# Stage one in the program's own order on ScalarE and VectorE, with the square written straight into the high half

## The chip, the cores and the metric

The kernel runs on one core of a Trainium2 chip. The metric is the time of one execution on the device in microseconds; for the kernel before, three executions have a median of 5993.0 us (5985.8 to 5993.41). The engines are named as in the profile: PE is TensorE's matrix multiply and PEld its weight load, DVE is VectorE, ACT is ScalarE, POOL is GpSimd, SP is SyncE, which here issues nearly all DMAs.

## The reference

Three computations run one after the other. The shapes are 8 batches of 3072 rows, 256 columns, and 64 columns for `z`.

```python
scores = (1.0 / S) * np.matmul(z, z.transpose(0, 2, 1))
attn = np.maximum(scores, 0.0) ** 2
x = (u * np.matmul(attn, v)).reshape(B * S, D)       # 24576 rows of 256
h = x @ w_in                                         # w_in: 256 x 2048, float64
x2 = np.maximum(0.01 * h, h) @ w_out                 # w_out: 2048 x 256, float64
# then: a gate gives every row of x2 to one of 8 experts, 3072 rows each,
# and each expert computes max(rows @ w1[e], 0) @ w2[e]
```

The third computation is the second stage of the kernel (`part_b`), which the change leaves alone.

## The kernel before

All matrix products are made of float32 data split into two halves that TensorE multiplies fast: `hi` is the value rounded on a copy to the type `float32r`, `lo` is the value minus `hi`, and a product is the sum of hi by hi, lo by hi and hi by lo. The helper `split` (line 336) does this: ScalarE copies into `hi` (line 337), VectorE subtracts for `lo` (line 338).

Stage one is `part_a`. Its work is 48 chunks of 512 rows, 6 to a batch. Each chunk has an attention half (class `Attn`) and an MLP half (class `Mlp`). The list `units` (lines 582 to 587) cuts them up: an attention half is 12 units of two key blocks each, an MLP half is 8 units of two blocks of 128 hidden columns each. The order is attention of chunk c, then the MLP of chunk c-1, then attention of chunk c+1, and so on; the very first two attention halves stand together.

Every unit has two parts. In `s1`, TensorE makes a tile of scores `s` (attention) or of hidden values `h` (MLP) in PSUM, and ScalarE and VectorE turn it into `hi` and `lo`. In `s2`, TensorE multiplies `hi` and `lo` into the accumulators `acc0` and `acc1`. The loop at line 647 calls `s1` of unit n and then `finish`, which calls `s2` of unit n-2, so the elementwise work of a unit has the matrix work of two other units beside it.

What ScalarE and VectorE do for one unit of attention: ScalarE writes `r` = relu of `s` (line 467). Then the square: in the first two chunks, and in 3 of 12 units (`k % 8 == 4`) of the others, by ScalarE in place (line 469); otherwise by VectorE as `s` times `r` (line 471). Then `split` into `hi` and `lo`. For one unit of the MLP: ScalarE writes 0.01 `h` (line 521), VectorE the maximum with `h` (line 522), then `split`.

Beside that there are smaller jobs, which come from `after` and `prefetch`, or before the loop: splitting the keys (`load_z`), the queries (`queries`) and the values (`load_v`) of chunks and batches to come, each behind a DMA; taking the accumulators out (`out_of`, lines 442 to 445, marked high priority); `ready`, which splits the result of attention for the MLP; and the gate's logits. The logits of a chunk are 32 VectorE instructions of line 575, two to an item of the list `side`, followed by one item of `rt.choose` with 5 small instructions; `after` takes three items at an MLP unit. In the first chunks `load_w` also converts the 16 pieces of the float64 weights to float32 by integer operations on VectorE (lines 375 to 381), two GpSimd operations (lines 382 and 383), ScalarE's high half and GpSimd's low half.

What sets the order. TensorE runs in the order in which the program calls it (`manual_schedule(engines={PE})`, line 841). The order on ScalarE, VectorE, GpSimd and the DMA queues is chosen by the scheduler of the framework when the kernel is built, from its own model of the times, under the dependencies between tiles; the order on an engine is then fixed, and at run time each engine takes its instructions one after the other.

Of the kernel before, what the change touches and what calls it, by code (L numbers as in the profile page):

```python
# [9 lines left out]
F32 = mybir.dt.float32  # L10
# [300 lines left out]
def part_a(nc, tc, uT, v, zT, w_in, w_out, wgT, x2d, L, rt):  # L311
# [12 lines left out]
    with ExitStack() as st:  # L324
# [20 lines left out]
        def load_w(piece):  # L345
            f, out = divmod(piece, 2)
            f *= 2
            W = cv.tile([128, 512], F32, name='cW')
# [11 lines left out]
            for half, c, x in src:  # L360
# [17 lines left out]
            V.scalar_tensor_tensor(W, lsw, 2.0 ** -52, P.bitcast(F32), op0=ALU.mult, op1=ALU.mult)  # L378

# [3 lines left out]
            nc.gpsimd.tensor_mul(W, W, P.bitcast(F32))  # L383
            split(hi, lo, W.rearrange("p (a d) -> p a d", **shape), nc.gpsimd)
# [17 lines left out]
        def load_z(b, g):  # L402
# [6 lines left out]
            split(k[:, 0], k[:, 1], zr)  # L409

        def queries(b, q):
# [6 lines left out]
            split(*x, zr)  # L418
            return x

        def load_v(b, g):
# [4 lines left out]
            split(vh, vl, raw)  # L426
            VH[b, g], VL[b, g] = vh, vl

        def halves(r):
            hi = wk.tile([128, 2, CH], F32R, tag='hi', name='hi', bufs=3)  # L430
            lo = wk.tile([128, 2, CH], F32R, tag='lo', name='lo', bufs=3)
            split(hi, lo, r)
            return hi, lo
# [8 lines left out]
        def out_of(acc, to):  # L442
            with tc.high_priority():
                nc.scalar.activation(to, acc[:, 1], AF.Copy)
                nc.vector.tensor_add(to, acc[:, 0], to)  # L445

        class Attn:

            def __init__(self, b, q):
                self.b, self.q = b, q  # L450
                self.xs, self.y = [], [None] * KT

            def prep(self):
                b, q = self.b, self.q
                self.z = Q.pop((b, q)) if (b, q) in Q else queries(b, q)

            def s1(self, k):
                if k == 0:
                    self.prep()
# [8 lines left out]
                if at.index(self) < 2 or k % 8 == 4:  # L468
                    nc.scalar.activation(r, r, AF.Square)
                else:  # L470
                    nc.vector.tensor_mul(r, s, r)  # L471
                return halves(r)

            def s2(self, k, hl, d):
# [13 lines left out]
                if k == NKB - 2:  # L488
                    self.y[d] = kv.tile([128, CH], F32, tag='raw', name='y', bufs=3)
                    out_of(self.acc[d], self.y[d])  # L490
                    if d == KT - 1:
                        for i, y in enumerate(self.y):
                            nc.vector.scalar_tensor_tensor(self.x[:, i], y, 1.0 / (S * S), self.x[:, i], op0=ALU.mult, op1=ALU.mult)
# [14 lines left out]
        class Mlp:  # L508
# [4 lines left out]
            def s1(self, f):  # L513
# [9 lines left out]
                return halves(r)  # L523

            def s2(self, f, hl, d):
# [12 lines left out]
                if f == FT - 2:  # L538
                    self.rows(d)

            def rows(self, d):
                if not lgt:
                    logit_tiles()
# [45 lines left out]
        Q = {(0, 0): queries(0, 0)}  # L589
        for g in range(NG):  # L590
            if g * G * 128 % CH == 0:
                load_z(0, g * G * 128 // CH)
            load_v(0, g)
            if g == 1:
                Q[0, 1] = queries(0, 1)
        q, piece = [], 0

        pending = []

        def finish():  # L600


            u, k, hl = q.pop(0)
            end = NKB if isinstance(u, Attn) else FT
            ends = end - 4 if isinstance(u, Mlp) else 0
            if k == ends:
                u.s2(k, hl, 0)
                pending.append((u, k, hl))
            else:
# [270 lines left out]
```

## Time and profile before

| | |
|---|---|
| median of three executions | 5993.0 us |
| the profiled execution | 6009.63 us |
| its span, first to last instruction | 6007.9 us |
| TensorE matmul busy (PE) | 5540.0 us, 92% |
| VectorE busy (DVE) | 3922.1 us, 65% |
| ScalarE busy (ACT) | 2739.6 us, 46% |
| GpSimd busy (POOL) | 497.0 us, 8% |
| mean granted TensorE clock | 0.968 |

In the rows further below, a line of a group names the line of the kernel, the engine, the operation, what it writes and reads, the shapes and the count; then the busy time in us and the mean duration of one in ns; then how long the engine was idle just before these instructions and which instruction ended that idle time. In a timeline, the first column is the start in us from the start of the span and the second the duration; a bracket at the end holds the idle time of the engine before the instruction and what ended it. `L436` is the helper `mm`, through which all matmuls of stage one go; an `x2` on a matmul is its pair for the two halves of the array.

### The profile page before, as it was taken

To read this page: it belongs to the slowest core of one execution; us is meant where nothing else is said; L and a number is where in the kernel's file an instruction comes from. 1 tells how busy PE (TensorE), PEld (TensorE's weight loads), DVE (VectorE), ACT (ScalarE), POOL (GpSimd) and SP (SyncE) were. 2 spreads that over 40 slices of the span, in tenths; PEclk is the share of its full clock that TensorE was granted. 3 is DMA by queue.
4 is the path that set the end of the run, shared out by engine and by line. 5 is a ranking of instruction groups with operands and counts; after the bars stand their busy time and mean duration, and the time that the engine had idled before them with its cause. 6 is when DMAs were issued, how large, how long until landed. Compare 5 with 4: busy or idle time off the path is not lost. (4 is left out here: it accounts for less than half of the span.)

```text
span 6007.9 us, 122714 instructions
## 1 busy us (share of the span) xinstructions
PE 5540.0 (92%) x53466; PEld 4782.2 (80%) x53466; DVE 3922.1 (65%) x8179; ACT 2739.6 (46%) x3172; POOL 497.0 (8%) x466
## 2 busy tenths in 40 slices
PE   5999999899989999999999999999998599999999
PEld 3877788787878778787787778878787488888898
DVE  8566666766666666666666666676666766767532
ACT  4555555555554555545555554555543122222232
POOL 5000000000000000000000000000000232323332
PEclk7999999999999999999999999999999799999999
DMA  3011110101111011111101111010110111111211
GB/s 105 21 33 43 33 30 25 54 17 33 33 43 33 17 42 35 32 33 34 42 17 33 47 29 33 22 54 19 31 31 15 40 53 50 57 50 55 70 46 36
DMA packets 147533, 229.19 MB, mean 38 GB/s; under 512 B 21936, under 2 KB 87472, under 8 KB 144816
## 3 DMA queue, kind: packets, MB, share of 16 engines
q1 hardware_dynamic: 124032, 153.15, 9.3%
q0 software_dynamic: 20736, 67.13, 3.2%
q8 instruction: 418, 6.85, 0.5%
q10 hardware_dynamic: 2224, 1.06, 0.1%
q14 instruction: 123, 1.01, 0.1%
HBM read 120.59 MB, written 50.33 MB: 28 GB/s over the span
## 5 line engine op out<-in xcount | busy, mean ns | idle before, releaser
L436 PE MATMUL acc<-lo,vh 64*128 64x512 f32 x4608 | 957.9, 408 | 209.3 <-DVE lo L338 209.2
L338 DVE TENSOR_TENSOR lo<-r,hi 128x1024 fp32r<-128x1024 f32 x576 | 707.1, 1228 | 556.2 <-ACT hi L337 556.2
L337 ACT ACTIVATE hi<-r 128x1024 fp32r<-128x1024 f32 x576 | 610.4, 1060 | 995.1 <-DVE r L471 989.0
L436 PE MATMUL acc<-hi,vh 64*128 64x512 f32 x4608 | 944.9, 403 | 74.7 <-DVE xt L445 36.2
L436 PE MATMUL acc<-hi,vl 64*128 64x512 f32 x4608 | 934.8, 398 | 0.0
L436 PE MATMUL acc<-woh,hi 64*128 64x256 f32 x6144 | 875.2, 281 | 0.8 <-DVE xt L445 0.6
L436 PE MATMUL acc<-woh,lo 64*128 64x256 f32 x6144 | 871.7, 280 | 0.2 <-DVE lo L338 0.2
L436 PE MATMUL acc<-wol,hi 64*128 64x256 f32 x6144 | 871.4, 280 | 0.0
L522 DVE TENSOR_TENSOR g<-h,g 128x1024 f32<-128x1024 f32 x384 | 469.9, 1224 | 447.7 <-ACT g L521 446.8
L436 PEld LDWEIGHTS acc<-lo,vh 64*128 64x128 f32 x4608 | 456.4, 191 | 373.6 <-DVE lo L338 291.1
L338 DVE TENSOR_TENSOR lo<-g,hi 128x1024 fp32r<-128x1024 f32 x384 | 470.5, 1225 | 421.8 <-ACT hi L337 421.8
L337 ACT ACTIVATE hi<-g 128x1024 fp32r<-128x1024 f32 x384 | 407.0, 1060 | 544.3 <-DVE g L522 543.5
L436 PE MATMUL h<-xh,wih 64*128 64x512 f32 x3072 | 611.1, 392 | 31.4 <-DVE g L522 31.4
L521 ACT ACTIVATE g<-h 128x1024 f32<-128x1024 f32 x384 | 393.7, 1025 | 503.6 <-PE h L436 503.1
L436 PEld LDWEIGHTS acc<-woh,hi 64*128 64x128 f32 x6144 | 587.4, 187 | 32.8 <-DVE y L445 18.0
L436 PEld LDWEIGHTS acc<-hi,vh 64*128 64x128 f32 x4608 | 458.1, 192 | 193.6 <-DVE xt L445 56.2
L436 PE MATMUL h<-xh,wil 64*128 64x512 f32 x3072 | 609.8, 391 | 0.0
L436 PE MATMUL h<-xl,wih 64*128 64x512 f32 x3072 | 606.5, 389 | 0.0
L436 PEld LDWEIGHTS acc<-wol,hi 64*128 64x128 f32 x6144 | 587.4, 187 | 13.2
L467 ACT ACTIVATE r<-s 128x1024 f32<-128x1024 f32 x576 | 583.0, 1012 | 12.2 <-PE s L436 12.2
L436 PEld LDWEIGHTS acc<-woh,lo 64*128 64x128 f32 x6144 | 587.3, 187 | 0.4 <-DVE lo L338 0.4
L767 ACT ACTIVATE bhi<-hb 128x512 fp32r<-128x512 f32 x384 | 228.7, 597 | 766.4 <-PE hb L764 579.5
(187 smaller groups left out, 9887.7 us busy)
## 6 DMA issues: line engine op xcount, KB each, us to landing
rawv<-in_v SPq DMA_DIRECT2D x96, 256.0 KB, 2.9
ut<-in_uT SPq DMA_DIRECT2D x48, 512.0 KB, 4.0
xh<-xh SPq DMA_DIRECT2D x192, 128.0 KB, 2.4
xl<-xl SPq DMA_DIRECT2D x192, 128.0 KB, 2.3
x_rows<-xt SPq DMA_DIRECT2D x48, 512.0 KB, 3.0
zq<-in_zT SPq DMA_DIRECT2D x96, 128.0 KB, 3.2
zr<-in_zT SPq DMA_DIRECT2D x96, 64.0 KB, 2.4
craw<-in_w_in SPq DMA_DIRECT2D x64, 64.0 KB, 2.3
```

The lines of the kernel that those rows point to most:

```text
L337: nc.scalar.activation(hi, src, AF.Copy)
L338: (eng or nc.vector).tensor_sub(lo, src, hi.bitcast(F32))
L436: nc.tensor.matmul(o, w[half], x[half], start=first, stop=last)
L467: nc.scalar.activation(r, s, AF.Relu)
L521: nc.scalar.activation(r, h, AF.Copy, scale=0.01)
L522: nc.vector.tensor_max(r, h, r)
L767: nc.scalar.activation(hi, h, AF.Relu)
```

## The change

It does three things, all in stage one.

First, ScalarE and VectorE join TensorE in the manual schedule: in stage one both run in the order in which the program calls them. SyncE's and GpSimd's orders stay with the scheduler.

Second, the loop is rewritten to that end. `s1` now only makes `r` (or `g`); a new method `halves` makes `hi` and `lo`. For unit n the order is: the loads due ahead (`ahead`), `s1` of n, `s2` of n-2, the first half of an accumulator that is done (`leave(0)`), `halves` of n, `leave(1)`, and then the small jobs that fall due (`todo`). Loads are split in two: the DMA is issued in `ahead`, and the function that it returns, the split, runs at the end of the next unit's work. The logits are taken at the MLP's units alone, one item between `hi` and `lo` in `halves`, two more in `todo`. A piece of weights is spread over four units, and its float32 buffer is doubled. The tables of the router (`rt.start`) and the gate's loads come at the seventh MLP unit.

Third, the square of chunks 2 to 47: ScalarE squares `r` straight into `hi` in every unit, VectorE squares `r` in place and then subtracts `hi` for `lo`. The separate square by ScalarE and its copy into `hi` are gone there, and VectorE no longer reads `s`.

The diff, with what the text speaks of:

```diff
         def load_w(piece):
-            W = cv.tile([128, 512], F32, name='cW')
+            W = cv.tile([128, 512], F32, name='cW', bufs=2)
...
+            yield
...
             V.scalar_tensor_tensor(W, lsw, 2.0 ** -52, P.bitcast(F32), op0=ALU.mult, op1=ALU.mult)
+            yield
...
             nc.gpsimd.tensor_mul(W, W, P.bitcast(F32))
+            yield
             split(hi, lo, W.rearrange("p (a d) -> p a d", **shape), nc.gpsimd)
...
-            split(k[:, 0], k[:, 1], zr)
+            return lambda: split(k[:, 0], k[:, 1], zr)
...
-            split(vh, vl, raw)
+            return lambda: split(vh, vl, raw)
...
                 nc.scalar.activation(r, s, AF.Relu)
-                if at.index(self) < 2 or k % 8 == 4:
+                return r
+
+            def halves(self, k, r):
+                hi, lo = new_halves()
+                if self.c < 2:
                     nc.scalar.activation(r, r, AF.Square)
+                    split(hi, lo, r)
                 else:
-                    nc.vector.tensor_mul(r, s, r)
-                return halves(r)
+                    nc.scalar.activation(hi, r, AF.Square)
+                    nc.vector.tensor_mul(r, r, r)
+                    nc.vector.tensor_sub(lo, r, hi.bitcast(F32))
+                return hi, lo
...
+            def halves(self, f, r):
+                hi, lo = new_halves()
+                nc.scalar.activation(hi, r, AF.Copy)
+                if f and side:
+                    side.pop(0)()
+                nc.vector.tensor_sub(lo, r, hi.bitcast(F32))
+                return hi, lo
...
+        def ahead(n, u, k):
+            i = k // 2
+            then = lambda step, f: todo.append((n + step, f))
+            if n < 2 * FT and (n % 2 or isinstance(u, Mlp)) and len(pieces) < FT:
+                w = load_w(len(pieces))
+                pieces.append(w)
+                next(w)
+                for step in (1, 2, 3):
+                    then(step, lambda: next(w, None))
+            if isinstance(u, Attn):
+                if u.c == 0:
+                    if i + 1 < NG:
+                        then(1, load_v(0, i + 1))
...
+                elif u.c > 1 and i in (3, 5):
+                    then(0, lambda: at[u.c - 1].ready(i // 4))
+                if u.q == NCH - 1 and u.b + 1 < B and i in (2, 4, 6, 8, 10, 11):
+                    then(1, load_v(u.b + 1, (i - 1) // 2))
                 return
+            for _ in range(2 if k else 0):
+                then(0, lambda: side and side.pop(0)())
+            if u.c == 0 and i == 6:
+                then(0, logit_tiles)
...
+            a = at[u.c + 1]
+            if i == 3 and a.c + 1 < len(at):
+                then(1, queries(at[a.c + 1].b, at[a.c + 1].q))
+            if a.q == NCH - 1 and a.b + 1 < B and i > 1:
+                then(1, load_v(a.b + 1, NG // 2 + i - 2))
+                then(1, load_z(a.b + 1, i - 2))
...
         for n, (u, k) in enumerate(units):
+            ahead(n, u, k)
+            r = u.s1(k)
+            out = finish() if len(q) > 1 else []
+            for f in out[:1]:
+                f()
+            q.append((u, k, u.halves(k, r)))
+            for f in out[1:]:
+                f()
+            for f in [f for m, f in todo if m <= n]:
+                f()
+            todo = [x for x in todo if x[0] > n]
...
-    with tc.manual_schedule(engines={mybir.EngineType.PE}):
+    with tc.manual_schedule(engines={mybir.EngineType.PE, mybir.EngineType.DVE, mybir.EngineType.Activation}):
         part_a(nc, tc, uT, v, zT, w_in, w_out, wgT, x2d, L, rt)
```

## Rows read from the trace of the kernel before

**Rows 1.** The page: busy time and share of the span of each engine.
```profile
PE 5540.0 (92%) x53466; PEld 4782.2 (80%) x53466; DVE 3922.1 (65%) x8179; ACT 2739.6 (46%) x3172; POOL 497.0 (8%) x466
```
**Rows 2.** Busy time of the engines in seven stretches.
```profile
core 0: us, PE busy (x) PEld busy (x) DVE busy (x) ACT busy (x) POOL busy (x), PEclk, DMA share, GB/s
321.00:361.70 40.70, 35.74 (x304) 27.58 (x302) 31.12 (x87) 22.97 (x24) 0.00 (x0) 1.00 0.07 21
361.70:406.50 44.80, 44.80 (x530) 39.64 (x528) 25.70 (x25) 19.87 (x23) 0.00 (x0) 1.00 0.06 13
406.50:413.60 7.10, 7.10 (x112) 6.84 (x110) 5.16 (x5) 4.53 (x6) 0.00 (x0) 1.00 0.58 152
6.00:145.70 139.70, 77.74 (x402) 53.84 (x404) 118.78 (x150) 65.97 (x85) 74.71 (x51) 0.72 0.34 101
145.70:221.20 75.50, 75.50 (x800) 65.00 (x800) 35.03 (x32) 46.89 (x49) 0.00 (x0) 1.00 0.12 30
150.00:4640.00 4490.00, 4227.31 (x44513) 3615.01 (x44510) 2989.37 (x5537) 2303.85 (x2491) 0.00 (x0) 0.98 0.12 32
4640.00:6008.00 1368.00, 1230.62 (x8519) 1109.82 (x8518) 811.30 (x2481) 364.81 (x592) 420.92 (x404) 0.95 0.15 50
```
**Rows 3.** Who PE waited for, 150 to 4640 us: total, times, longest.
```profile
PE acc L436 <- DVE lo L338: 188.9, 151, 2.8
PE acc L436 <- DVE xt L445: 36.8, 47, 0.8
PE h L436 <- DVE g L522: 31.4, 8, 5.5
```
**Rows 4.** Timeline around a gap of PE in chunk 3's attention half.
```profile
334.93 0.42 DVE L575 SCALAR_TENSOR_TENSOR junk<-xt,wg 128x256 bf16<-128x256 f32 x1
...
337.43 1.22 DVE L338 TENSOR_TENSOR lo<-r,hi 128x1024 fp32r<-128x1024 f32 x1
...
338.70 0.49 PE L436 MATMUL acc<-lo,vh 64*128 64x512 f32 x2 [2.79 <-DVE lo L338]
```
**Rows 5.** DVE's logits in the attention half from 321.0 to 361.7 us, grouped.
```profile
L575 DVE SCALAR_TENSOR_TENSOR junk<-xt,wg 128x256 bf16<-128x256 f32 x32 | 11.4, 416 | 0.0
```
**Rows 6.** TensorE's first `s2` matmul of a unit, where nothing stalls: units 0, 2, 6.
```profile
149.94 0.39 PE L436 MATMUL acc<-hi,vh 64*128 64x512 f32 x2
...
156.74 0.39 PE L436 MATMUL acc<-hi,vh 64*128 64x512 f32 x2
...
170.34 0.39 PE L436 MATMUL acc<-hi,vh 64*128 64x512 f32 x2
```
**Rows 7.** ACT's first result tile `y`, chunk 2 (280.8) to chunk 47 (4549.72).
```profile
L444 ACT ACTIVATE y<-acc x92: 577/586/595, 280.8 to 4550.2; 128x512 f32<-128x512 f32 x92
...
4549.72 1.07 ACT L444 ACTIVATE y<-acc 128x512 f32<-128x512 f32 x2
```
**Rows 8.** Durations of the elementwise operations, grouped by line and shape, whole span.
```profile
L338 DVE TENSOR_TENSOR lo<-r,hi 128x1024 fp32r<-128x1024 f32 x576 | 707.1, 1228 | 556.2 <-ACT hi L337 556.2
...
L467 ACT ACTIVATE r<-s 128x1024 f32<-128x1024 f32 x576 | 583.0, 1012 | 12.2 <-PE s L436 12.2
...
L471 DVE TENSOR_TENSOR r<-s,r 128x1024 f32<-128x1024 f32 x414 | 504.3, 1218 | 0.3 <-ACT r L467 0.3
...
L469 ACT ACTIVATE r<-r 128x1024 f32<-128x1024 f32 x162 | 171.9, 1061 | 5.0
...
L338 DVE TENSOR_TENSOR vl<-rawv,vh 128x512 fp32r<-128x512 f32 x96 | 69.1, 727 | 36.7 <-ACT vh L337 36.7
```
**Rows 9.** A batch boundary: timeline at the longest gap of PE.
```profile
580.65 0.63 ACT L337 ACTIVATE vh<-rawv 128x512 fp32r<-128x512 f32 x1 [3.10 <-DMA rawv<-in_v]
...
585.26 0.80 PE L436 MATMUL h<-xh,wih 64*128 64x512 f32 x2 [5.34 <-DVE g L522]
```
**Rows 10.** The start: two weight pieces in ScalarE's timeline.
```profile
73.60 0.63 ACT L337 ACTIVATE wih<-cW 128x512 fp32r<-128x512 f32 x1 [2.55 <-POOL cW L383]
...
80.85 0.63 ACT L337 ACTIVATE woh<-cW 128x512 fp32r<-128x512 f32 x1 [5.70 <-POOL cW L383]
```

More of the change, by code (lines that the diff above doesn't have):

```diff
@@ L417, in queries @@
             x = [wk.tile([128, CH], F32R, tag='x%s0' % n if b == q == 0 else 'q' + n, name='q' + n, bufs=1) for n in 'hl']
-            split(*x, zr)
-            return x
+            Q[b, q] = x
+            return lambda: split(*x, zr)
         def load_v(b, g):
@@ L425, in load_v, with new_halves @@
             vl = kv.tile([128, G, D], F32R, tag='vl', name='vl', bufs=NG)
-            split(vh, vl, raw)
             VH[b, g], VL[b, g] = vh, vl
[L429 to L433, printed above, removed]
+            return lambda: split(vh, vl, raw)
+        def new_halves():
+            return [wk.tile([128, 2, CH], F32R, tag=n, name=n, bufs=3) for n in ('hi', 'lo')]
         def mm(o, w, x, half, first, last):
@@ L487, in s2, with leave @@
                             mm(self.acc[d][:, j], w[:, i, c], a[:, i], half, k + i == n == 0, k + i == NKB - 1 and n == 2)
[L488 to L493, printed above, removed]
+            def leave(self, d):
+                y = self.y[d] = kv.tile([128, CH], F32, tag='raw', name='y', bufs=3)
+                out_of(self.acc[d], y)
+                if d == KT - 1:
+                    for i, y in enumerate(self.y):
+                        nc.vector.scalar_tensor_tensor(self.x[:, i], y, 1.0 / (S * S), self.x[:, i], op0=ALU.mult, op1=ALU.mult)
+                    if self.c in (0, len(at) - 1):
+                        for i in range(KT):
+                            self.ready(i, self.c > 0)
             def ready(self, k, last=False):
@@ L537, in s2, with leave @@
                                    f + i == FT - 1 and t % 2 == 1 and n == 2)
[L538 to L543, printed above, removed]
+            def leave(self, d):
                 lp, wg, j0 = lgt['pool'], lgt['wg'], self.c * TT
@@ L587, in part_a @@
         units += later
[L589 to L598, printed above, removed]
+        q, pending, todo, Q = [], [], [], {}
         def finish():
             u, k, hl = q.pop(0)
[L604 to L607, printed above, removed]
+            att = isinstance(u, Attn)
+            u.s2(k, hl, 0)
+            if k == (0 if att else FT - 4):
@@ L647, in part_a @@
[L647 to L657 removed]
+                return []
+            if pending:
+                w, j, h = pending.pop()
+                w.s2(j, h, 1)
@@ new lines, in part_a @@
+        pieces = []
+        for f in [queries(0, 0), load_z(0, 0)]:
+            f()
+        for f in (load_v(0, 0), load_z(0, 1)):
+            todo.append((0, f))
+        for n, (u, k) in enumerate(units):
+            ahead(n, u, k)
[7 more added lines that the diff above has]
+            for f in [f for m, f in todo if m <= n]:
+                f()
+            todo = [x for x in todo if x[0] > n]
@@ L658, in part_a @@
         while q:
-            finish()
+            for f in finish():
+                f()
         while side:
```

65 lines of the change are left out of this document (13 added, 52 removed).

## The prediction

> **What bounds the kernel now.** I read the busy shares first: TensorE's matmuls cover 92% of the span, VectorE 65%, ScalarE 46% [rows 1]. So TensorE sets the pace, and the question is where it stands still. The table of stretches answers that: from 150 to 4640 us PE is busy for 4227 of 4490 us; the second stage, behind 4640 us, is not touched by the change and keeps its 1368 us [rows 2]. The same table cuts one chunk: 40.7 us of attention half with 5.0 us in which PE is not even busy, then 44.8 us and 7.1 us with no idle time at all [rows 2]. All the loss of an ordinary chunk lies in the attention half.
>
> The waits say who is late: in stage one PE waited 188.9 us for VectorE's `lo`, 151 times, and 36.8 us for `xt`, once a chunk [rows 3]. The timeline shows why `lo` is late. Around the longest gap of a chunk VectorE does not idle: it works through logits (line 575), starts `lo` only at 337.43, and PE goes on at 338.70 after 2.79 us [rows 4]. In that attention half stand all 32 logits, 11.4 us [rows 5]. The scheduler put them, and the emptying of the accumulator behind some of them, ahead of work for which TensorE waits. Nothing is short of capacity: VectorE is busy for 25.7 of the MLP half's 44.8 us [rows 2].
>
> **What a chunk costs without stalls.** Units 0 to 6 of a stretch with no stall have their first `s2` matmul at 149.94 and 170.34: 3.40 us for an attention unit [rows 6]. The window of 40.7 us holds the matmuls of ten units, 34.0 us; so it loses 6.7 us, and the chunk of 92.6 us (40.7 + 44.8 + 7.1) could take 85.9 [rows 2, 6]. The mean chunk is longer than 92.6: from the first `y` of chunk 2 to that of chunk 47 are 45 chunks, (4549.72 - 280.8) / 45 = 94.86 us [rows 7]. The 2.2 us of difference are the batch boundaries (below) and a granted clock of 0.98 in the mean over the stage, against 1.00 in the chunk shown [rows 2]. In the start, where PE stands still for much of the time, the mean is 0.72, so part of it is spent at the lower of the two levels, 1.2 GHz [rows 2]; I take it that the lower level goes with the stalls.
>
> **The change, part by part.**
>
> The order of the logits. 16 items of two logits, 0.71 us each (11.4 / 16, [rows 5]), leave the attention half for the MLP half, one item between `hi` and `lo`, two behind the unit. VectorE's work in the MLP half becomes 25.7 + 11.4 + about 1 (`choose`) = 38 of 44.8 us [rows 2, 5]: it fits. In the attention half it becomes 31.1 - 13.9 (logits with their accumulator reads, and `choose`) + 3.7 (below) = 20.9 us for ten units of 3.40: it fits with a third to spare. So the 6.7 us go, if the fixed order makes no new wait.
>
> The square. Three units of twelve lose a ScalarE square of 1.06 us and gain a VectorE one of 1.22 [rows 8]: 3.7 us more on VectorE in a chunk, off TensorE's path. The chain of a unit was relu 1.01, square 1.22 on VectorE, `hi` 1.06, `lo` 1.23, together 4.5. It stays as long: VectorE squares `r` in place, and must wait until ScalarE has read it for `hi`; so again relu 1.01, `hi` 1.06, square 1.22, `lo` 1.23 [rows 8]. With four handovers of some 0.1 us I take 4.9. TensorE asks for it two units later, 6.8 us from the end of `s1` to `hi` (149.94 to 156.74) and about 0.45 more to `lo` [rows 6]: 2.3 us to spare. `s` in PSUM comes free earlier, since only the relu reads it; TensorE did not wait for that, so nothing is gained. The bounds of this edit are 0 and, if the chain came out of its cover, what it exceeds 7.2 us by.
>
> The fixed order. Each engine now holds what stands behind a waiting instruction. `leave(0)` stands ahead of `halves` on ScalarE, and waits for an `s2` that ends about 1.4 us after `s1`; relu covers 1.0 of it. Queued behind are `hi` and with it `lo`: 0.4 us late, out of 2.3 spare. `leave(1)` waits for the end of the unit's matmuls, when the next relu isn't due yet. At the end of the MLP the chain is tighter, since two short attention units follow, but by then the logits are used up (17 items, three at each unit after the first). I take no stall for an ordinary chunk; the upper bound, from the chunk's waits that don't concern logits, is 1 us.
>
> The batch boundary, 7 times. The values and keys of the next batch were split by ScalarE in a row, each behind its DMA: ScalarE held the MLP's relu back, and PE stood for 5.34 us [rows 9]; that wait came 8 times, 31.4 us in all [rows 3]. Now each MLP unit from the third takes one value and one key tile, with the DMAs issued a unit ahead on SP, but only three `raw` buffers. VectorE gets six value splits at 0.73 us [rows 8] and six key splits, which are half as large, at some 0.4: 38 + 6.8 = 44.8 us, as much as the MLP half lasts. So there the cover is used up. Between 0 and the roughly 10 us that such a chunk exceeds others by now, I take 3 us, near the lower end, since the work just fits: 7 x 3 = 21 us.
>
> The start. To 145.7 us PE is busy for 77.7 of 139.7 us at a granted clock of 0.72; from there to 221.2 it has no idle time [rows 2]. What blocks is ScalarE: it sat 5.70 us at a weight piece behind GpSimd [rows 10] with the relu of a unit behind it. With the pieces spread over four units each that chain runs beside the rest. The next limit is VectorE: 118.8 + 35.0 = 153.8 us of work up to 221.2 [rows 2], all of which remains. TensorE needs 75.5 us plus some 13 units of 3.40, 120. So stage one reaches the same point at 6 + 154 = 160 us instead of 221 if VectorE binds throughout (61 saved), at 127 if TensorE does (94). I take 60. At the worst SP, whose queue carries nine issues for each pair of pieces and the loads of values between, holds the splits back in fixed order, and 30 are left. The router's tables and the gate's loads move from the first microseconds to the seventh MLP unit; a few us, in that range.
>
> **The sum.** 46 chunks x (94.86 - 85.9) = 412 us; less 21 for the boundaries; plus 60 at the start: 451 us. Against the profiled execution's own 6009.6 us that makes 5559; this execution lies 16.6 us above the median of 5993.0, to which I apply the same gain: 5542 us. Its own bounds: all at best 412 + 94, 5487; all at worst 412 - 70 - 46 + 30 = 326, 5667.
>
> **The rivals.**
>
> Loads block the fixed order (A). ScalarE and VectorE in order stop at each split whose DMA is late, at the start and the boundaries; ordinary chunks gain, nothing else does. For it: one late split already stopped everything for 5 us [rows 9], and three buffers serve all loads. Against: loads are now issued a unit ahead and spread. 412 - 70 = 342 us gained: 5651.
>
> The gap is a matter of buffers (B). `r` and `s` have two buffers, `hi` and `lo` three; if these bound, a new order would leave the gaps. Only the start gains: 5993 - 60 = 5933. Against it: with the same buffers six units run without a stall [rows 6], and the wait ends with a `lo` that was queued, not one without room. The Trainium skill ("Perfetto Trace Analysis", section "Identifying the Most-Contended Engine" and what follows on strategy) has this as a rule: the same gap, repeated, can mean that there is no room for the next tile. The trace doesn't bear it out here.
>
> The MLP half becomes serial (C, slower). Place: the fixed order of VectorE and ScalarE in an MLP unit, with the logits in it. If max waits for ScalarE, `hi` for max, `lo` for `hi`, and nothing of another unit fills these waits, a unit takes 1.0 + 1.2 + 1.1 + 1.2 and three items, 2.1: 6.6 us, with the chunk's other jobs some 7.0, where TensorE needs 5.6 (44.8 / 8). Eight units lose 11 us, a chunk takes 97.1, and 46 x (97.1 - 94.86) - 60 = +43: 6036. It decides from 6.9 us a unit on. Against it: one item stands just where VectorE waits for `hi`, and relu and max belong to a unit that TensorE needs only two units later.
>
> The change doesn't do what it says (D): the order built is in effect the old one: 5993.
>
> **Chances.** Forecast 0.76, A 0.14, B 0.04, C 0.03, D 0.03. The range takes the forecast's own bounds and A: 5487 to 5680, 0.9 of the chance. A measurement of this kernel can tell 0.2%, 12 us, from no change. Faster is forecast, A and B, 0.94; same is D, 0.03; slower is C, 0.03.
>
> **What would show it.** Right: the same stretches of an attention half with PE busy throughout; no wait of PE for `lo` worth 10 us in all of stage one; logits between MLP operations; first `y` of one chunk to the next at about 86 us; granted clock near 1.00 there; the stretch of 75 us that ends the start reached some 60 us earlier. Wrong: waits of ScalarE for `rawv` or `zr` with PE idle behind them (A), gaps at the same units ended by a `lo` that started late though VectorE was free (B), PE waiting for `g` in every MLP unit (C). I would be most wrong by a stall that the new order makes in every unit: each 0.1 us of that is 0.1 x 20 x 46 = 92 us.

## The result and the profile after

The changed kernel takes 5559.9 us (median of four runs, 5557.7 to 5563.9) where the kernel before, beside it, takes 5991.5: a ratio of 0.928, 95% interval 0.9266 to 0.9298. The prediction was 5542 us in a range of 5487 to 5680; the forecast's case came, and no rival. The profiled executions differ by 6007.9 - 5560.2 = 447.7 us of span, where the sum of the prediction said 451. That agreement is better than its terms, and in part luck: one of them was a third too large, and another part was not foreseen.

Where the time went can be cut at two points that both traces have, the first and the last start of VectorE's part in emptying the MLP's accumulator (`xt`). Before, in the view of the tile `xt` (duration of one at least, in the middle and at most, then the first and the last start):

```profile
L445 DVE TENSOR_TENSOR xt<-acc,xt x96: 679/681/693, 227.9 to 4635.7; 128x512 f32<-128x512 f32 x96
```

And after:

```profile
L445 DVE TENSOR_TENSOR xt<-acc,xt x96: 681/683/692, 189.0 to 4199.6; 128x512 f32<-128x512 f32 x96
```

| part | before, us | after, us | gained | predicted |
|---|---|---|---|---|
| start, to the first `xt` | 227.9 | 189.0 | 38.9 | 60 |
| chunks, to the last `xt` | 4407.8 | 4010.6 | 397.2 | 412 - 21 = 391 |
| rest, mostly the second stage | 1372.2 | 1360.6 | 11.6 | 0 |

The busy shares, which answer [rows 1]: TensorE rises from 92% to 97% of a shorter span, and VectorE does more, not less, since it took over squares.

```profile
PE 5375.5 (97%) x53466; PEld 4707.5 (85%) x53466; DVE 4100.0 (74%) x8317; ACT 2644.1 (48%) x3034; POOL 501.6 (9%) x466
```

The table of stretches, which answers [rows 2]: the three pieces of an ordinary chunk (7.1 us from its first unit to its third, 34.1 us of ten attention units, 44.6 us of MLP half), then a batch boundary's MLP half, then the start in two pieces and all chunks.

```profile
core 0: us, PE busy (x) PEld busy (x) DVE busy (x) ACT busy (x) POOL busy (x), PEclk, DMA share, GB/s
1904.50:1911.60 7.10, 7.10 (x112) 6.84 (x110) 4.42 (x5) 5.51 (x6) 0.00 (x0) 1.00 0.01 2
1911.60:1945.70 34.10, 34.10 (x306) 28.18 (x306) 26.56 (x24) 22.46 (x23) 0.00 (x0) 1.00 0.26 71
1945.70:1990.30 44.60, 44.60 (x532) 39.77 (x530) 35.07 (x91) 17.59 (x19) 0.00 (x0) 1.00 0.06 19
...
489.80:534.50 44.70, 44.23 (x568) 39.93 (x564) 39.22 (x102) 24.14 (x33) 0.00 (x0) 1.00 0.21 61
...
6.00:106.20 100.20, 80.47 (x592) 61.20 (x592) 86.53 (x98) 78.28 (x94) 40.33 (x25) 0.95 0.38 112
106.20:181.70 75.50, 61.71 (x610) 51.36 (x612) 65.12 (x92) 31.24 (x37) 37.71 (x27) 0.91 0.16 47
181.70:4150.00 3968.30, 3955.21 (x43082) 3440.98 (x43080) 3101.72 (x5557) 2147.47 (x2291) 0.00 (x0) 1.00 0.13 36
```

In an ordinary chunk PE is busy from end to end, at 2.4 GHz, the upper of the clock's two levels. The ten attention units take 34.1 us, where the prediction said 34.0 and the kernel before took 40.7, and a chunk takes 7.1 + 34.1 + 44.6 = 85.8 us. The waits of PE, which answer [rows 3] (total, times, longest; from 183 to 4160 us), show what is left of 188.9 us for `lo`: nothing of attention's, and 3 us of the MLP's.

```profile
PE acc L437 <- DVE xt L445: 9.9, 7, 2.1
PE acc L437 <- DVE lo L538: 3.1, 8, 0.8
```

The timeline of VectorE in an MLP unit, which answers [rows 4]: the logits (now line 587) stand between the maximum and `lo`, where VectorE would wait for `hi` anyway; after two of them there are still 0.44 us of that wait.

```profile
1961.85 1.22 DVE L530 TENSOR_TENSOR g<-h,g 128x1024 f32<-128x1024 f32 x1
1962.99 0.41 DVE L587 SCALAR_TENSOR_TENSOR junk<-xt,wg 128x256 bf16<-128x256 f32 x1
...
1964.20 1.23 DVE L538 TENSOR_TENSOR lo<-g,hi 128x1024 fp32r<-128x1024 f32 x1 [0.44 <-ACT hi L535]
```

### The profile page after: what moved, and what is told of

Its sections match the earlier page's. It is cut to its first block, busy times and chain, and to the rows that moved or that the text cites. A ratio compares the mean times of both kernels' runs of the same rounds, so it can differ in the third digit from the quotient of the medians.

```text
span 5560.2 us, 122841 instructions
## 1 busy us (share of the span) xinstructions
PE 5375.5 (97%) x53466; PEld 4707.5 (85%) x53466; DVE 4100.0 (74%) x8317; ACT 2644.1 (48%) x3034; POOL 501.6 (9%) x466
## 5 line engine op out<-in xcount | busy, mean ns | idle before, releaser
L474 DVE TENSOR_TENSOR r<-r 128x1024 f32<-128x1024 f32 x552 | 676.5, 1226 | 358.1 <-ACT hi L473 350.0
L437 PE MATMUL acc<-hi,vh 64*128 64x512 f32 x4608 | 902.9, 388 | 14.1 <-DVE xt L445 9.9
L437 PE MATMUL acc<-hi,vl 64*128 64x512 f32 x4608 | 902.1, 388 | 10.4 <-DVE vl L338 10.4
L437 PE MATMUL acc<-lo,vh 64*128 64x512 f32 x4608 | 902.8, 388 | 4.5 <-DVE lo L338 4.4
L463 ACT ACTIVATE r<-s 128x1024 f32<-128x1024 f32 x576 | 591.7, 1027 | 418.6 <-DVE r L474 314.4
L475 DVE TENSOR_TENSOR lo<-r,hi 128x1024 fp32r<-128x1024 f32 x552 | 676.6, 1226 | 56.1 <-DVE r L474 2.3
L473 ACT ACTIVATE hi<-r 128x1024 fp32r<-128x1024 f32 x552 | 585.8, 1061 | 114.5 <-PE acc L437 99.9
L783 DVE SCALAR_TENSOR_TENSOR blo<-hb,bhi 128x512 fp32r<-128x512 f32 x384 | 264.3, 689 | 401.2 <-ACT bhi L782 347.8
```

What stands on the lines that cost most here:

```text
L437: nc.tensor.matmul(o, w[half], x[half], start=first, stop=last)
L463: nc.scalar.activation(r, s, AF.Relu)
L473: nc.scalar.activation(hi, r, AF.Square)
L474: nc.vector.tensor_mul(r, r, r)
L475: nc.vector.tensor_sub(lo, r, hi.bitcast(F32))
L783: nc.vector.scalar_tensor_tensor(lo, h, 0.0, hi.bitcast(F32), op0=ALU.max, op1=ALU.subtract)
```

## The experiments

The kernels were timed in four sittings, each with the kernel before beside them: the result first, then the experiments from "scheduler's order" to "logits at once", those from "relu twice" to "weights without GpSimd", and last the table's other three together with "changed, again". The kernel before took 5991, 5989, 5960 and 6008 us in them (on record for the last three are chips 6, 6 and 13). So the table gives the ratio to the kernel before in the same sitting, and the last `xt` of the profiled run, the end of stage one. Where an expectation names microseconds without naming what they are held against, they are meant beside the 5991; on that scale (ratio times 5991.5) the run with relu twice takes 5573 us, the two with more work on VectorE 5606 and 5887, and the one without GpSimd 5544.

What follows stage one goes with the sitting and not with the kernel: in the profiled runs it takes 1359 to 1366 us in the second sitting, 1327 to 1332 in the third and 1370 to 1376 in the fourth, though nothing was changed there. The 11.6 us of the rest in the table above are therefore not shown to be an effect of the change. The changed kernel ran in two sittings, and there stage one ends at 4199.6 and 4201.8 us; so I take the end of stage one to compare runs to about 2 us.

| kernel | us | ratio to before, interval | last `xt`, us |
|---|---|---|---|
| before | 5991.5 | 1 | 4635.7 |
| changed | 5559.9 | 0.9282, 0.9266 to 0.9298 | 4199.6 |
| changed, again | 5574.6 | 0.9278, 0.9265 to 0.9291 | 4201.8 |
| new program, scheduler's order | 6080.2 | 1.0147, 1.0130 to 1.0164 | 4719.1 |
| old program, fixed order | 5952.0 | 0.9931, 0.9914 to 0.9947 | 4586.8 |
| old square | 5588.9 | 0.9324, 0.9309 to 0.9340 | 4222.6 |
| logits at once | 6105.8 | 1.0187, 1.0170 to 1.0204 | 4744.4 |
| relu twice | 5545.4 | 0.9302, 0.9288 to 0.9317 | 4213.1 |
| VectorE 4.8 us more a chunk | 5577.2 | 0.9357, 0.9343 to 0.9371 | 4245.6 |
| VectorE 9.7 us more a chunk | 5857.1 | 0.9826, 0.9811 to 0.9841 | 4529.4 |
| weights without GpSimd | 5516.9 | 0.9253, 0.9240 to 0.9265 | 4185.8 |
| keys earlier | 5551.8 | 0.9243, 0.9230 to 0.9256 | 4179.4 |
| both of these | 5541.1 | 0.9222, 0.9210 to 0.9235 | 4164.5 |
| piece in one unit | 5639.1 | 0.9383, 0.9370 to 0.9396 | 4264.2 |

The changed kernel once more, in the last sitting, beside the last three of the table:

> The changed kernel itself once more, beside the other three on the same chip, so that they can be held against it directly; its ratio to the kernel before should be 0.928 again, by every theory.

### Order or program: which of the two parts carries the gain?

First the new program with the order left to the scheduler:

```diff
-    with tc.manual_schedule(engines={mybir.EngineType.PE, mybir.EngineType.DVE, mybir.EngineType.Activation}):
+    with tc.manual_schedule(engines={mybir.EngineType.PE}):
```

> The changed kernel with one line taken back: only TensorE is held to the program's order, ScalarE and VectorE go back to the scheduler's. The new program (logits called at MLP units, loads split in two, new square) stays. My theory: the scheduler is free to pull logits ahead of lo again, so most of the 8.6 us a chunk come back; 5850 to 5960 us, with PE waiting for lo in the attention half, though the logits' place in the program may pull it down somewhat. Rival (the loop and the place of the logits in it do the work, the fixed order adds nothing): 5550 to 5590 us.

It came out at 6080 us, beyond my theory's interval and 1.5% above the kernel before. The waits of PE from 221 to 4670 us:

```profile
PE acc L437 <- DVE lo L475: 281.7, 138, 4.9
PE h L437 <- DVE g L530: 44.1, 9, 6.6
```

Given the choice, the scheduler again puts VectorE's small work ahead of `lo`, although the program now calls it at the MLP's units. In an attention half all 32 logits of a chunk stand within 1873 to 1890 us (VectorE grouped from 1868 to 1905 us), and PE waits behind them:

```profile
L587 DVE SCALAR_TENSOR_TENSOR junk<-xt,wg 128x256 bf16<-128x256 f32 x32 | 11.5, 424 | 0.0
```

```profile
1892.79 0.79 PE L437 MATMUL acc<-lo,vh 64*128 64x512 f32 x2 [4.50 <-DVE lo L475]
```

So where the program calls the logits makes no difference that would help. The scheduler also lacks something here that it had in the old program: the new one no longer marks the emptying of the accumulators as high priority. The waits listed are for `lo` and `g`, not for `xt`, but how much of the 1.5% that mark is worth was not tried. The start is lost too: the first `xt` starts at 225.2 us, before the change 227.9.

Then the old program with the order fixed:

```diff
-    with tc.manual_schedule(engines={mybir.EngineType.PE}):
+    with tc.manual_schedule(engines={mybir.EngineType.PE, mybir.EngineType.DVE, mybir.EngineType.Activation}):
```

> The kernel before with one line changed: ScalarE and VectorE held to the order of the old program, in which three logit items stand behind each MLP unit and the loads of a batch are split where they are issued. My theory: the logits leave the attention half by that alone, so ordinary chunks fall from 94.9 to 86 to 88 us, while the start and the batch boundaries, where a split stands right behind its DMA, get no better or worse by some 50 us: 5600 to 5750 us. Rival (the old program's order is only usable with the rewritten loop): ScalarE and VectorE stop behind waits in every unit, and the time is 5950 us or more.

It gained 0.7%, so the rival was right as to the time. But half of my theory stands: PE's waits for `lo` fall from 188.9 to 15.4 us, and another has come in its place, once a chunk (waits of PE from 270 to 4540 us):

```profile
PE acc L436 <- DVE xt L445: 176.3, 46, 5.4
PE acc L436 <- DVE lo L338: 15.4, 28, 0.8
```

The timeline of VectorE and of PE at one of them shows why. In the old loop, `s1` of a unit with its whole elementwise work stands ahead of `s2` of the unit two before, and the emptying of the accumulator behind that. So VectorE squares (471), waits for `hi`, makes `lo`, and only then adds the accumulator's halves, for which PE has stood still:

```profile
2128.24 1.22 DVE L471 TENSOR_TENSOR r<-s,r 128x1024 f32<-128x1024 f32 x1
2130.92 1.23 DVE L338 TENSOR_TENSOR lo<-r,hi 128x1024 fp32r<-128x1024 f32 x1 [1.46 <-ACT hi L337]
2132.07 1.28 DVE L445 TENSOR_TENSOR xt<-acc,xt 128x512 f32<-128x512 f32 x2
```

```profile
2132.89 0.51 PE L436 MATMUL acc<-hi,vh 64*128 64x512 f32 x2 [3.89 <-DVE xt L445]
```

The changed loop puts `leave(0)` ahead of `halves`, which is just this point; that line was not tried by itself. The start of the old program is worse in fixed order as well (first `xt` at 277.9 us); there it splits loads where it issues them.

So neither part brings the gain by itself: old program and scheduler's order 1, fixed order alone 0.993, new program alone 1.015, both 0.928.

### Is it the logits' place?

The changed kernel, with all items of `side` taken in a row in `leave(1)` of the MLP, right after they are put there:

```diff
+                while side:
+                    side.pop(0)()
```

> The changed kernel, all fixed orders kept, with all 17 items of a chunk (32 logits and choose, some 13 us of VectorE) taken in one row as soon as the MLP's result is out, in the next attention half. My theory (the place of the logits is what cost the time before): VectorE is 13 us late there, of which 2 to 5 us are covered, so a chunk loses 8 to 11 us: 5930 to 6070 us, about the kernel before. Rival (the fixed order as such, or the new square, carries the gain, not the logits' place): 5560 to 5620 us.

6106 us: with every other part of the change in place, the logits' place alone gives back more than the whole gain. PE waits at one place in a chunk, as this row shows, and 46 such waits make 440.2 us, 9.6 each:

```profile
1872.03 0.80 PE L437 MATMUL acc<-lo,vh 64*128 64x512 f32 x2 [9.47 <-DVE lo L475]
```

I expected 8 to 11 us a chunk; the ends of stage one, 4744.4 - 4199.6, say 544.8 / 46 = 11.8. The part above 9.6 I put down to the clock, of which the last section tells. Here the logits stand in one row, in the kernel before they stood spread out; so the run shows that their place can cost this much, and the waits of [rows 3 and 4] that it did cost there.

### Does the square matter, and has the chain of a unit room?

```diff
+                self.s = s
...
-                if self.c < 2:
+                if self.c < 2 or k % 8 == 4:
                     nc.scalar.activation(r, r, AF.Square)
-                    split(hi, lo, r)
                 else:
-                    nc.scalar.activation(hi, r, AF.Square)
-                    nc.vector.tensor_mul(r, r, r)
-                    nc.vector.tensor_sub(lo, r, hi.bitcast(F32))
+                    nc.vector.tensor_mul(r, self.s, r)
+                split(hi, lo, r)
```

> The changed kernel with the old rule for the square (VectorE multiplies s and r in 9 of 12 units, ScalarE squares in place in 3, then both halves are split off). My theory: the chain of a unit stays inside its cover of 7.2 us either way (relu, square, hi, lo on one path is again about 4.9 us), so the time is within 0.3% of the changed kernel: 5545 to 5580 us. Rival (the new square carries part of the gain, because hi no longer waits for VectorE's square and s comes free earlier): at least 1 us a chunk more, 5610 us or above.

It takes 0.5% more than the changed kernel (0.9324 against 0.928), between the two theories: stage one is 22 us longer. In ordinary chunks nothing changes, from one to the next 85.8 us against 85.7; but at each boundary two chunks, with 87.5 and 89.2 us, together lose 3 us more than the changed kernel's, 7 x 3 = 21. The new square is thus no part of the steady gain, but it is worth some 20 us where the engines are late. A likely reason is that `hi` no longer waits for VectorE. On the page of this kernel ScalarE is idle for 650.9 us before `hi`, nearly always for VectorE's square:

```profile
L337 ACT ACTIVATE hi<-r 128x1024 fp32r<-128x1024 f32 x576 | 610.9, 1061 | 650.9 <-DVE r L472 587.6
```

In the changed kernel that wait is gone from `hi` (line 473), which waits 99.9 us for PE's accumulator. But part of it has moved: ScalarE's relu (line 463), which waits 9.2 us in the kernel with the old square and never for VectorE, now waits 314.4 us for VectorE's square. That `hi` is what the boundaries gain from was not tried.

For the room in the chain, relu twice in chunks 2 to 47:

```diff
                 nc.scalar.activation(r, s, AF.Relu)
+                if self.c > 1:
+                    nc.scalar.activation(r, s, AF.Relu)
```

> The changed kernel; in chunks 2 to 47 ScalarE does each relu of attention twice, so the chain of every attention unit is 1.03 us longer and ScalarE has 12.4 us more work a chunk. My theory (the chain has 2.3 us to spare: in the trace of the changed kernel lo ends at 1924.08 us, and TensorE comes to it at about 1926.4): ordinary units cost nothing, at most the first two units of a half, where ScalarE also empties the accumulators, lose 1 to 1.5 us; 5550 to 5630 us. Rival (the chain has no cover, the new order has made it the bound): 1 us in ten units of 46 chunks, 5790 us or more.

Stage one ends 11 to 14 us later (4213.1), and an ordinary chunk still takes 85.75 us. The cost lies at the boundaries, 1 to 2.5 us each, where PE's waits for `xt` (from 183 to 4170 us) have doubled:

```profile
PE acc L437 <- DVE xt L445: 19.3, 7, 3.6
```

So the chain does have at least 1.03 us to spare in each of twelve units, as predicted; my 1 to 1.5 us for the first two units of a half was too much.

### Has VectorE room in the MLP half?

Some work that nobody waits for, once in a unit, and in the second kernel twice (`range(2)`):

```diff
+            lgt['xx'] = lp.tile([128, 2, D], F32, name='xx')
...
                 nc.vector.tensor_sub(lo, r, hi.bitcast(F32))
+                if f and lgt:
+                    for _ in range(1):
+                        nc.vector.tensor_max(lgt['xx'], lgt['wg'][:, :2], lgt['wg'][:, 2:4])
```

> The changed kernel with one further VectorE instruction of about 0.69 us (128x512 float32) in each of 7 MLP units of a chunk, in work that nobody waits for. My theory (VectorE has 38 of 44.8 us to do in the MLP half, 44.8 of 44.8 at a batch boundary): 4.8 us more still fit in an ordinary chunk, and only the 7 boundaries lose up to 4.8 us each and the start a few: 5565 to 5605 us. Rival (VectorE has much room there, also at the boundaries): within 0.2% of the changed kernel, 5550 to 5571 us. Rival (VectorE binds in every chunk): 46 x 4.8, about 5780 us.

> The same with two such instructions in each of 7 MLP units, 9.7 us a chunk. My theory: 38 + 9.7 = 47.7 us of work in 44.8, so 1 to 3 us in each of 46 chunks, and about 8 us at each of 7 boundaries: 5650 to 5760 us. Rival (room): 5550 to 5590 us.

With 4.8 us more, stage one is 45 us longer: an ordinary chunk takes 86.2 instead of 85.7 us, a boundary 92.4 instead of 88. That is my theory with a little more at each place. With 9.7 us more it is 329 us longer, far more than the 1 to 3 us a chunk that I had from sums of busy time; ordinary chunks take 91 to 93 us, those at a boundary 97 to 100. From the second kernel, the row of PE at the end of an MLP half, then VectorE's `lo` in one of that half's units, then three stretches: the half, the unit from one maximum of VectorE to the next, and the time behind the half:

```profile
1951.99 0.50 PE L438 MATMUL s<-qh,K 64*128 64x512 f32 x2 [2.00 <-DVE g L531]
```

```profile
1941.06 1.23 DVE L539 TENSOR_TENSOR lo<-g,hi 128x1024 fp32r<-128x1024 f32 x1 [0.44 <-ACT hi L536]
```

```profile
core 0: us, PE busy (x) PEld busy (x) DVE busy (x) ACT busy (x) POOL busy (x), PEclk, DMA share, GB/s
1900.00:1946.70 46.70, 46.70 (x548) 41.45 (x546) 39.04 (x94) 16.84 (x19) 0.00 (x0) 1.00 0.01 2
1938.71:1944.91 6.20, 6.20 (x88) 5.71 (x86) 5.72 (x19) 1.98 (x2) 0.00 (x0) 1.00 0.01 3
1953.30:1960.10 6.80, 6.21 (x58) 5.91 (x58) 5.24 (x6) 4.02 (x5) 0.00 (x0) 0.50 0.01 4
```

Over the half VectorE is busy for 39.0 of 46.7 us, which looks like room. But the half is not loaded evenly: most of the idle time lies at its first two units (1.81, 1.13 and 1.84 us). In a unit that carries logits a round of VectorE (maximum, wait for `hi`, `lo`, small work) takes 6.20 us, of which 5.72 are work and 0.44 the wait for `hi`, where PE needs 5.62 (the step between its units in the changed kernel). So the work alone is already a little too much for such a unit, and the wait in the fixed order comes on top. VectorE falls behind by about 0.6 us a unit; PE notices only where the short attention units come, then stands still there three times within 7 us (0.73, 2.00 and 0.59 us) and goes on at half the clock. With one instruction more instead of two, such rounds take 5.47 us and PE's 5.62 still covers them. That is rival C's place, though its round was to be long by waiting and this one is so mostly by work; it begins to cost between 0.7 and 1.4 us more in a unit.

### What held the batch boundaries and the start?

At a boundary of the changed kernel, the timeline of VectorE and one row of ScalarE:

```profile
532.60 1.23 DVE L475 TENSOR_TENSOR lo<-r,hi 128x1024 fp32r<-128x1024 f32 x1
533.75 0.69 DVE L338 TENSOR_TENSOR vl<-rawv,vh 128x512 fp32r<-128x512 f32 x1
534.35 0.42 DVE L338 TENSOR_TENSOR K<-zr,K 128x256 fp32r<-128x256 f32 x1
534.77 0.69 DVE L445 TENSOR_TENSOR xt<-acc,xt 128x512 f32<-128x512 f32 x1
```

```profile
532.92 0.42 ACT L337 ACTIVATE K<-zr 128x256 fp32r<-128x256 f32 x1 [1.16 <-DMA zr<-in_zT]
```

The last value and the last key stand ahead of the emptying of the accumulator, for which PE waits 1.16 us there, and the key is late by its own DMA. Moving five of the six key loads into the attention half ahead:

```diff
+                if u.q == NCH - 1 and u.b + 1 < B and i in (3, 5, 7, 9, 11):
+                    then(1, load_z(u.b + 1, (i - 3) // 2))
...
-                then(1, load_z(a.b + 1, i - 2))
+                if i == 2:
+                    then(1, load_z(a.b + 1, NCH - 1))
```

> The changed kernel; of the six key loads of a batch boundary five (DMA and split) move from the MLP half into the attention half ahead of it. My theory (at a boundary VectorE is full in the MLP half, so what lies there late delays the next attention half by 2.3 to 4.6 us; the attention half has room): the boundaries come down from 88.0 to 90.3 us to 86 to 87 us, together 8 to 18 us less than the changed kernel. Rival (the wait is the DMA's own time behind a late issue, or the buffers of the loads, and moves with them): no change, within 5 us, or a new wait in the attention half.

It gained more than my theory said: beside the changed kernel in the same sitting 5551.8 us against 5574.6, 22.8 us less, and the chunks at boundaries take 85.7 us like all others. All that is left of PE's waits from 183 to 4140 us is one:

```profile
PE acc L437 <- DVE lo L538: 0.8, 1, 0.8
```

For the start, the weights without GpSimd:

```diff
-            nc.gpsimd.tensor_add(W, T.bitcast(F32), W)
-            nc.gpsimd.tensor_mul(W, W, P.bitcast(F32))
+            V.tensor_add(W, T.bitcast(F32), W)
+            V.tensor_mul(W, W, P.bitcast(F32))
...
-            split(hi, lo, W.rearrange("p (a d) -> p a d", **shape), nc.gpsimd)
+            split(hi, lo, W.rearrange("p (a d) -> p a d", **shape))
```

> The changed kernel; the three GpSimd operations of each of the 16 weight pieces (add, multiply, low half) go to VectorE. My theory (in the start, VectorE's instructions that lie beside a GpSimd one are stretched by about 1.1 us, three a piece, 16 x 3.3 = 53 us, which is why the start gained 40 us and not 60): VectorE takes on about 16 x 2 = 32 us and loses the 53, so the start gets 10 to 25 us shorter, 5535 to 5550 us, and no VectorE low half there takes 2.3 us any more. Rival (GpSimd's help is real, the stretched instructions are not its doing): VectorE has 32 us more, 5575 to 5595 us.

The first `xt` comes at 174.2 us instead of 189.0. VectorE's instructions from 6 to 182 us, grouped; first the changed kernel:

```profile
L338 DVE TENSOR_TENSOR lo<-r,hi 128x1024 fp32r<-128x1024 f32 x24 | 39.4, 1640 | 12.4 <-ACT hi L337 12.4
L377 DVE TENSOR_SCALAR cT<-craw 128x512 int32<-128x512 int32 x16 | 18.8, 1173 | 0.0
...
L383 DVE TENSOR_SCALAR cP<-craw 128x512 int32<-128x512 int32 x16 | 14.4, 897 | 0.0
...
L445 DVE TENSOR_TENSOR y<-acc,y 128x512 f32<-128x512 f32 x4 | 2.7, 681 | 0.0
```

and without GpSimd:

```profile
L338 DVE TENSOR_TENSOR lo<-r,hi 128x1024 fp32r<-128x1024 f32 x24 | 29.3, 1220 | 9.5 <-ACT hi L337 9.5
...
L386 DVE TENSOR_TENSOR cW<-cW,cP 128x512 f32<-128x512 f32 x16 | 11.1, 692 | 0.6
...
L383 DVE TENSOR_SCALAR cP<-craw 128x512 int32<-128x512 int32 x16 | 6.7, 421 | 0.0
L377 DVE TENSOR_SCALAR cT<-craw 128x512 int32<-128x512 int32 x16 | 6.7, 420 | 0.0
```

The same instructions on the same shapes take 1640 and 1220 ns, 1173 and 420, 897 and 421. These three groups give VectorE 29.9 us back (10.1 + 12.1 + 7.7), and smaller ones some 11 more (line 378 falls from 15.0 to 11.1 us, `K` from 5.8 to 2.5). Its 48 new instructions of 0.69 us cost 33 us. So GpSimd's help was worth less than nothing to VectorE, by some 8 us. ScalarE no longer waits for GpSimd either: it had sat 61.0 us of the first 180 before the change, at pieces like those of [rows 10], and 18.2 us after it (12.3 before `wih`, 5.9 before `woh`). How the 15 us are shared between the two is not told apart.

What the spreading of a piece over several units is worth:

```diff
-                for step in (1, 2, 3):
+                for step in (1, 1, 1):
```

> The changed kernel with the steps of a weight piece no longer spread over three units: conversion, GpSimd's add and multiply and the split all stand at the end of one unit. My theory (in a fixed order ScalarE stops where it waits for GpSimd, and the relu and hi of the next unit stand behind it): ScalarE waits for GpSimd's two operations, 1.6 + 1.5 us, in each of 16 pieces, and the start gets 20 to 50 us longer. Rival (VectorE's total of work alone sets the start): within 5 us of the changed kernel.

It cost more than I said: the first `xt` comes at 253.5 us, 64 us later and later than before the change (227.9). The waits of ScalarE from 6 to 180 us, for GpSimd:

```profile
ACT wih L337 <- POOL cW L386: 41.3, 6, 6.9
ACT woh L337 <- POOL cW L386: 34.5, 5, 6.9
```

The wait for a piece is not only the 3.1 us of GpSimd's two operations, as I had counted, but up to 6.9 us, as VectorE's conversion of the same piece now stands right ahead of them; and the relu of the next unit stands behind it.

Both improvements together (the weights without GpSimd, the keys earlier):

> The GpSimd operations of the weight pieces on VectorE and the earlier key loads together. If both theories hold their gains add, since one lies in the first 180 us and the other at the boundaries: 22 to 35 us less than the changed kernel, so a ratio to the kernel before of about 0.923. If the two share a cause, it is no better than the better of the two, some 16 us less.

They add up: stage one ends 37.3 us earlier than in the changed kernel of the same sitting, where the earlier keys alone gave 22.4 and the start about 15. The whole takes 5541.1 us against 5574.6, 33.5 us or 0.6% less. This version beats both kernels.

## Why the prediction was right, and where not

**What bounded the kernel.** Right: the loss was VectorE's order, not its capacity [rows 2 to 4]. The run with the logits at once shows it from the other side. One reading was too low: VectorE's work in the attention half, put at 20.9 us, measured 26.6 of 34.1; ten squares and ten `lo` at 1.22 and 1.23 us alone are 24.5. It fits still, with a fifth to spare and not a third.

**An ordinary chunk.** The step "85.9 us without stalls" measured 85.7 to 85.8, and the chunks together gained 397 us where the terms 412 - 21 say 391. The six units without a stall [rows 6] were the right yardstick for the other ten. The mean of 94.86 [rows 7] was to be explained by boundaries and clock; that was right too. Counted over the clock's records between the first and the last `xt`, the trace of before has the half clock in 42 stretches, together 157 us, which is worth at most half of that, 78 us. After, it has two such stretches, 6.8 us.

**The square.** Right in ordinary chunks (no cost, no gain); that it would help at the boundaries was not foreseen. The 2.3 us to spare were read correctly enough: 1.03 us more were not felt.

**The fixed order.** "No stall for an ordinary chunk" came true. But the reason given for the MLP half, 38 of 44.8 us of VectorE, is no measure of its room. The busy time was 35.1 of 44.6, and by that sum 9.7 us more would have been 0.2 too much; they cost 7 us a chunk. What counts is the length of one unit's round, work and wait together, in the units that carry most.

**The batch boundary.** The size was right, 2.3 to 4.6 us against 3. The reason was not: VectorE was busy for 39.2 of 44.7 us there, not for 44.8. Late were a key's DMA and what stood behind it in the order; and three rounds there, at 5.8 to 6.4 us, were longer than 5.62. The two are not told apart, as the earlier loads removed both.

**The start.** This is the term that was mis-sized: 60 against 38.9. The step that failed is "if VectorE binds throughout". The work was as predicted, 86.5 + 65.1 = 151.7 us to 181.7 against 153.8; but VectorE did not work throughout: some 24 of the 175.7 us behind the first 6 it stood still, 12.4 of them waiting for attention's `hi`. And part of its work was waiting for GpSimd in disguise, which [rows 2] had counted as work: in the kernel before, the VectorE instruction of line 381 already took 1201 ns in the mean there, and 428 in the kernel without GpSimd. The bound of 30 for the worst case covered it.

**The sum.** 39 + 397 + 12 = 448 against 451 predicted: the start's 21 us too much were made good by 6 in the chunks and by 12 of the rest, which differs from sitting to sitting by more than that; so that the sum comes within 3 us is luck. The prediction's 5542 lies 18 us below the measured median mostly because the profiled execution of before lay 16.6 us above its median, and I carried its whole gain over.

**The rivals.** B and D are ruled out by the result (nothing about the buffers of `r`, `s`, `hi` and `lo` was changed). A is present in small: in the chunks ScalarE waits 8 times for a key's DMA, 12.7 us in all, and not at each load. C's place is real: with 1.4 us more in a unit it binds, with 0.7 hardly.

## What to carry to other kernels

Where the busiest engine waits for one that is itself busy, look at what that engine did just before: here it was small work that nobody waited for, and moving it into that engine's own wait, in a program that keeps it there, was worth most of 7%. An order fixed by hand pays only with a program written for it, with what frees a buffer ahead of what can wait and each load split from its use; the fixed order alone gave 0.7%, the new program alone lost 1.5%. How much more such an order holds is read from the length of a round in the fullest unit, work and wait, not from the busy share of a longer stretch.

## What the runs showed of the chip

**A stop of TensorE costs more than itself.** In the old program with the fixed order, PE stands for 3.89 us and then runs at the lower level of its clock, 1.2 GHz, for more than 3 us, though it is busy without a break:

```profile
core 0: us, PE busy (x) PEld busy (x) DVE busy (x) ACT busy (x) POOL busy (x), PEclk, DMA share, GB/s
2128.00:2132.00 4.00, 1.00 (x12) 0.52 (x8) 2.54 (x3) 2.17 (x4) 0.00 (x0) 1.00 0.01 2
2134.30:2137.60 3.30, 3.30 (x19) 3.30 (x18) 2.73 (x10) 1.68 (x2) 0.00 (x0) 0.50 0.45 157
```

Each of the 46 waits of the run with the logits at once shows it as well, with 10.2 us or more at the half level that begin while PE still stands; of its 11.8 us a chunk, 9.6 are the wait. In the kernel before, the clock fell in about half the chunks behind a gap like that of [rows 4], but not in the chunk shown there, and in others behind shorter gaps or at a boundary.

A wait also costs something at full clock. Around the gap of [rows 4] the neighbours of the matmul shown there are:

```profile
335.52 0.40 PE L436 MATMUL acc<-hi,vl 64*128 64x512 f32 x2
...
339.04 0.40 PE L436 MATMUL acc<-hi,vh 64*128 64x512 f32 x2
```

The starts are 3.18 us (335.52 to 338.70) and 0.34 us (to 339.04) apart, where pairs that follow each other without a wait start 0.23 us apart. So 3.06 us are lost where the profile lists 2.79 as idle, since one matmul lasts 0.39 us and the next starts before it has ended. Between the first and the last `xt`, PE's idle time falls from 260.9 to 12.9 us, by 248; the busy time of the same matmuls falls from 4146.9 to 3997.7, by 149, of which the half clock explains at most 75 and such restarts some 60, by the starts around the waits of both traces. A stall that is removed thus gives back more than the wait that the profile lists.

**VectorE beside GpSimd.** In the changed kernel's trace one can see which of two instructions is held up. Two `lo` of VectorE and the GpSimd instructions beside them:

```profile
24.11 1.67 POOL L385 TENSOR_TENSOR cW<-cT,cW 128x512 f32<-128x512 f32 x1 [22.14 <-DVE cW L380]
24.55 2.32 DVE L338 TENSOR_TENSOR lo<-r,hi 128x1024 fp32r<-128x1024 f32 x1
...
29.62 1.21 DVE L338 TENSOR_TENSOR lo<-r,hi 128x1024 fp32r<-128x1024 f32 x1
...
30.16 1.82 POOL L338 TENSOR_TENSOR wil<-cW,wih 128x512 fp32r<-128x512 f32 x1 [0.74 <-ACT wih L337]
```

The first `lo` starts 0.44 us behind a GpSimd instruction and takes 1.1 us longer than the second, about what GpSimd still needed (1.23 us); the second starts ahead of GpSimd. It is so throughout: of the 21 `lo` here that overlap a GpSimd instruction, the 11 that start behind it take 1.81 to 2.32 us, the 10 that start ahead of it 1.21 to 1.23. `y<-acc,y`, with one input in PSUM, takes 681 ns in the mean with GpSimd at work and 683 without. The Trainium skill ("SBUF — State Buffer", section "Who interferes with whom") has a rule for this: a VectorE instruction with two inputs in SBUF contends with a GpSimd instruction that reads SBUF, over ports that the two engines share and that are an exclusive lock. The times above agree with it, and with GpSimd's part gone `lo` fell from 1640 to 1220 ns in the mean. The instructions of lines 377 and 383 have one input in SBUF and are stretched as well, which the sentence on two inputs does not cover.
